# A fused attention, routed-expert and gated-layer kernel: the first keys' queue, four zero matmuls, routing's maxima, one gather's transposes, a split yload and an earlier conversion

## The chip, the core and the metric

The kernel runs on one core of a Trainium2 chip. The metric is device microseconds (us) from the first to the last instruction of one execution with its surroundings; the median of several runs is compared. The core has five engines with their own instruction queues: TensorE (PE, with its weight loads listed apart as PEld), VectorE (DVE), ScalarE (ACT), GpSimd (POOL) and SyncE (SP, which here only asks for DMA transfers). Rows of the profile give times from the start of the span; L12 is line 12 of the kernel before.

## What is computed

Three stages in a row, on 8 batches of 8 heads with 576 tokens and head size 64, so 4608 tokens of 512 features:

```python
a = softmax(phi, axis=2)                      # 8 x 8 x 576 x 32
k_m = einsum('bhsm,bhsd->bhmd', a, k)         # 32 memory rows for each head
v_m = einsum('bhsm,bhsd->bhmd', a, v)
attn = softmax(q @ k_m.T / 8) @ v_m           # x: 4608 x 512

logits = normalised(x) @ normalised(expert_emb).T / tau
e = argmax(logits); gate = softmax(logits)[e]
out = gate * (relu(x @ w1[e]) @ w2[e])        # 8 experts, 512 -> 1024 -> 512

g = out @ w_gate                              # 512 -> 1536
result = (silu(g) * (out @ w_val)) @ w_out    # 1536 -> 512
```

The weights of the last stage arrive as 64-bit floats; all else is 32-bit.

## The kernel before

**Attention (0 to about 240 us).** Batches run staggered, 16 us apart. For one batch: `fetch` (L216) asks SP for phi, k, v and q, four DMAs for each tensor (L223); `weigh` (L245) makes the softmax of phi over the tokens (maxima on VectorE at L251, transposes L257 on TensorE, the subtraction L268, the exponentials on ScalarE at L271); `memory` (L285) multiplies the weights with k and v (L296), then VectorE builds the divisor (L303, L304), a masked copy rm (L306) and the scaled keys km (L313, L314), which TensorE transposes (L320); `queries` (L352) transposes q (L360, L362); `scores` (L370) and `attend` (L405) follow, with the long matmuls at L446 and the copies X<-x at L447. GpSimd's L403 divides the attention weights in one large operation.

**Routing.** For every second batch `route` (L463) takes the maxima of the logits (L479 to L483 on VectorE), makes a one-hot of the expert (L487) and counts tokens of each expert on TensorE (L491 to L493). `table` turns the counts into 37 slots of 128 tokens, each of one expert.

**Main slots (about 240 to 690 us, 12.5 us each).** `moe` (L734): `gather` fetches the 128 rows of a slot (L745), `trx` (L801) transposes them on TensorE (L806) and splits them into a high part xh (ScalarE, L809) and a low part xl (VectorE, L810); `split` (L781) does the same with the expert's weights (w1h L785, w1l L786) where the expert changes; `l1` (L813) multiplies (L820), `trh` (L828) transposes and splits the hidden row (L835 to L839, low part hl), `l2` (L841) multiplies again (L848), `put` (L851) scales and scatters the rows (L854 to L856). A product is made of three matmuls, high by high, high by low and low by high. In the shadow of the slots a converter (L660) turns the 64-bit weights into 32-bit ones, a unit at a time, on VectorE and GpSimd (L666 to L674), and stores them. In slots 17, 19 and 21 `yload` (L1090) prepares 256 rows of the gated layers each: transposes, sums L1104, and then the same split in two parts, L1110 to L1113 for the sources and L1115, L1116 for four sums of them.

**Gated layers (about 690 to 1550 us).** Six blocks of 768 tokens; `fload` (L984) asks for converted weights F, `fsplit` splits them into G0h and G0l (L993, L994), `product` multiplies (L1009), `after` and `both` combine (L1018 to L1055), the sigmoid is at L1046.

**What sets the order.** All instructions are issued in an order written out by hand. In the attention each step is a generator with a due time (`CFG`, one list for each step; `todo` is sorted by it); `moe`'s list says when its first steps come, `warm` is a list of [time, n] for n calls of `busy` (L179), a matmul of zeros into a bank that nobody reads. From slot 1 on, the loop at L906 issues a slot's steps in its own order, with `cv` giving how many conversion units a slot gets. So no planner stands between the code and the queues: an engine does its instructions in the order of the code.

## Time and profile before

| | us |
|---|---|
| median of three timed runs | 1557.24 |
| the three runs | 1557.24, 1552.91, 1561.06 |
| profiled execution, whole | 1552.55 |
| its span, first to last instruction | 1550.8 |
| TensorE busy in it | 1492.7 (96%) |
| mean granted clock of TensorE | 0.976 |

A busy row adds up the durations of an engine's instructions. TensorE's clock is given as granted share: 1.00 is 2.4 GHz, 0.50 is 1.2 GHz. In a timeline row `[1.73 <-DVE km L313]` means that the engine stood idle for 1.73 us before the instruction and that the one named ended last of what it waited for; SPq is SP's queue, in which an issue of a DMA takes the time given. The rows that the prediction uses stand in a section of their own below.

### The profile page before, as it was taken

The page shows a single profiled execution, that of the slowest core. Times are in us where ns is not written, and L with a number is a line of the kernel's source. Part 1 is how long each engine was busy: PE and PEld are TensorE (multiplying, and loading weights), DVE is VectorE, ACT ScalarE, POOL GpSimd, SP SyncE. Part 2 cuts the span into 40 slices and gives each one's busy share as a digit, 9 for nine tenths or more (in the row PEclk, how much of TensorE's full clock was granted, in tenths as well). Part 3 has the DMA queues.
Part 4 walks back from the last instruction along what each step waited for, and adds up shares of the span by engine and source line. Part 5 has one row for each costly group of instructions (what it writes and reads, how often), then busy time and mean ns, then how long its engine had stood idle before and what let it go on. Part 6 is the DMA issues. An engine that isn't in the chain of part 4 may idle for free.

```text
span 1550.8 us, 24891 instructions
## 1 busy us (share of the span) xinstructions
PE 1492.7 (96%) x8362; PEld 1322.8 (85%) x8362; DVE 968.3 (62%) x1632; ACT 706.5 (46%) x1238; POOL 547.4 (35%) x430
## 2 busy tenths in 40 slices
PE   7988789999999999999999999999999999999997
PEld 5777668888877888888988998999899889989996
DVE  5788646856586456635666666566656656765662
ACT  2465653333353242425554554454455444545542
POOL 2345533533332333322243234324332442343233
PEclk8799889999999999999999999999999999999999
DMA  9797535555663364525325323432343244324311
GB/s 311 238 285 174 163 83 188 145 185 169 221 234 118 123 229 148 205 85 197 119 79 179 121 103 93 183 119 89 132 158 111 90 155 142 106 83 168 118 42 54
DMA packets 114527, 230.55 MB, mean 149 GB/s; under 512 B 11021, under 2 KB 62488, under 8 KB 114384
## 3 DMA queue, kind: packets, MB, share of 16 engines
q1 hardware_dynamic: 104368, 200.01, 39.4%
q0 software_dynamic: 10016, 28.81, 5.7%
q8 instruction: 67, 1.10, 0.3%
q14 instruction: 76, 0.62, 0.1%
HBM read 311.67 MB, written 43.21 MB: 229 GB/s over the span
## 4 chain that ended last, share of the span: by engine, by line
PE 66%; DMA 1%; ACT 0%; issue 0%; DVE 0%; another core or an unknown queue 0%; POOL 0%; POOLq 0%; ACTq 0%
PE s L1009 10%; PE k L1009 10%; PE x L1009 10%; PE s L820 5%; PE x L848 5%; PE t L1009 5%; PE k L1201 2%; PE k L1202 2%; PE x L1202 2%; PE k L1200 2%; PE x L1201 2%; PE x L1200 2%; PE s L1201 2%; PE s L1200 2%; PE s L1202 2%; PE t L1100 1%
## 5 line engine op out<-in xcount | busy, mean ns | idle before, releaser
L994 POOL TENSOR_TENSOR G1l<-F,G1h 128x768 fp32r<-128x768 f32 x71 | 140.2, 1975 | 321.6 <-ACT G1h L993 321.5
L1189 POOL TENSOR_TENSOR wo<-wos,wo 128x512 fp32r<-128x512 f32 x72 | 117.4, 1638 | 197.1 <-ACT wo L1188 197.1
L994 DVE TENSOR_TENSOR G0l<-F,G0h 128x1024 fp32r<-128x1024 f32 x72 | 94.2, 1308 | 113.1 <-ACT G0h L993 112.9
L1192 DVE TENSOR_TENSOR uh<-u,uh 128x768 fp32r<-128x768 f32 x72 | 108.0, 1506 | 65.8 <-ACT uh L1191 65.8
L839 DVE TENSOR_TENSOR hl<-t,hh 128x512 fp32r<-128x512 f32 x74 | 47.6, 686 | 118.8 <-ACT hh L838 118.5
L848 PE MATMUL x<-w2h,hh 128*128 128x512 f32 x288 | 117.0, 406 | 0.0
L848 PE MATMUL x<-w2l,hh 128*128 128x512 f32 x288 | 114.2, 396 | 0.0
L848 PE MATMUL x<-w2h,hl 128*128 128x512 f32 x288 | 114.2, 396 | 0.0
L826 ACT ACTIVATE hs<-s 128x512 f32<-128x512 f32 x74 | 40.3, 596 | 145.1 <-PE s L820 138.4
L856 POOL DMA_INDIRECT yd<-y,yi x37 | 40.2, 1088 | 178.7 <-ACT hh L838 128.6
L820 PE MATMUL s<-w1l,xh 128*128 128x512 f32 x296 | 95.1, 403 | 7.7 <-DVEq L783 4.1
L820 PE MATMUL s<-w1h,xh 128*128 128x512 f32 x296 | 97.7, 412 | 2.5 <-ACTq L783 2.5
L820 PE MATMUL s<-w1h,xl 128*128 128x512 f32 x296 | 94.2, 400 | 0.0
L670 POOL TENSOR_TENSOR ca<-ca,cr 128x512 int32<-128x512 int32 x36 | 50.6, 1405 | 116.3 <-DVE cr L669 115.1
L854 ACT ACTIVATE y<-x,tg 128x512 f32<-128x512 f32 x36 | 24.8, 690 | 137.0 <-PE x L848 129.2
L1188 ACT CAST wo<-wos 128x512 fp32r<-128x512 f32 x72 | 45.1, 627 | 67.9 <-PE s L1202 47.8
L993 ACT CAST G0h<-F 128x1024 fp32r<-128x1024 f32 x72 | 75.7, 1052 | 0.7 <-DMA F<-wst 0.5
L820 PEld LDWEIGHTS s<-w1l,xh 128*128 128x128 f32 x296 | 56.7, 193 | 22.7 <-DVEq L783 5.4
L1035 DVE TENSOR_TENSOR u<-u,sg 128x768 f32<-128x768 f32 x72 | 54.4, 755 | 32.9 <-ACT sg L1046 32.9
L1018 ACT COPY s<-s 128x384 f32<-128x384 f32 x72 | 34.6, 481 | 79.8 <-PE s L1009 79.8
L820 PEld LDWEIGHTS s<-w1h,xl 128*128 128x128 f32 x296 | 56.4, 190 | 13.9
L993 ACT CAST G1h<-F 128x768 fp32r<-128x768 f32 x72 | 60.4, 839 | 12.0 <-PE s L1009 12.0
(308 smaller groups left out, 4535.9 us busy)
## 6 DMA issues: line engine op xcount, KB each, us to landing
rw<-in_moe_w_dram SPq DMA_DIRECT2D x296, 512.0 KB
F<-wst SPq DMA_DIRECT2D x71, 896.0 KB
wos<-woc SPq DMA_DIRECT2D x72, 256.0 KB
yt<-yd SPq DMA_DIRECT2D x36, 260.0 KB
xs<-X SPq DMA_DIRECT2D x32, 256.0 KB
cr<-in_moe_w_gate_dram SPq DMA_DIRECT2D x12, 512.0 KB
cr<-in_moe_w_val_dram SPq DMA_DIRECT2D x12, 512.0 KB
wst<-cs SPq DMA_DIRECT2D x12, 512.0 KB
```

What stands on the lines that cost most here:

```text
L670: G.tensor_tensor(out=a, in0=a, in1=lo, op=ALU.add)
L820: PE.matmul(ph[nh], lhsT=l[:, c, :], rhs=r[:, 512 * nh:512 * nh + 512], start=(c == 0 and r is wh and l is xh), stop=(c == KD - 1 and l is ...
L848: PE.matmul(py, lhsT=l[:, c % 4, :], rhs=r, start=(c == 0 and l is hh and r is wh), stop=(c == KF1 - 1 and l is hl))
L993: A.copy(out=h, in_=src)
L994: (G if part and i else V).tensor_tensor(out=l, in0=src, in1=h.bitcast(F32), op=ALU.subtract)
L1009: PE.matmul(pg, lhsT=w[:, k, o], rhs=y[:, RHS[n], k], start=(n in (1, 5, 2) and k == j == 0), stop=(last and k == 1 and j == 2), skip_grou ...
L1035: mul = lambda o, x, y: V.tensor_tensor(out=o, in0=x, in1=y, op=ALU.mult)
L1189: G.tensor_tensor(out=wl, in0=w, in1=wh.bitcast(F32), op=ALU.subtract)
L1192: V.tensor_tensor(out=ul, in0=u, in1=uh.bitcast(F32), op=ALU.subtract)
L1200: PE.matmul(po[t], lhsT=uh[:, cols], rhs=wh, start=(f == 0), stop=False)
L1201: PE.matmul(po[t], lhsT=uh[:, cols], rhs=wl, start=False, stop=False)
L1202: PE.matmul(po[t], lhsT=ul[:, cols], rhs=wh, start=False, stop=(f == NF2 - 1))
```

## The change

Eight edits:

1. The first batch's four k loads are asked for by ScalarE instead of SP; the v loads come next on SP. Other batches are as before.
2. The last entry of `warm` goes from no matmul to four, at −3.86 instead of −20.
3. Two steps of `route` and one of `setup` get later times.
4. Two of `moe`'s first steps go from 104.8 to 108.3: the first slot's `trx`.
5. `cv` gives two units to slots 27 and 30, so that the last of the 37 is done one slot sooner; a second unit of a slot is issued behind the splits.
6. `yload` in slots 17, 19 and 21 is issued in two pieces: the second (L1115 and L1116) behind the next slot's splits.
7. A sigmoid of one column at the end of slot 35.
8. In the first block of the gated layers the split of the next weights is issued ahead of `both(0, 6)`.

```diff
@@ -91,9 +91,9 @@
                             -18.88, -18.88, -15.02],
                  'queries': [-23.63, -23.63, -21.09, -20.21, -19.61],
                  'weigh': [-50.65, -44.65, -42.01, -39.92, -35.01],
-                 'route': [17.41, 23.24, 26.4, 29.17, 30.73, 30.73, 33.02, 34.16, 35.64, 35.64, 35.64, 35.64, 42.66,
+                 'route': [17.41, 23.24, 29.15, 29.17, 31.9, 31.95, 33.02, 34.16, 35.64, 35.64, 35.64, 35.64, 42.66,
                            42.66, 44.07, 44.95, 46.72]},
-        'setup': [-100.87, -100.87, -41.81, -30.12, -26.83],
+        'setup': [-100.87, -50.0, -41.81, -30.12, -26.83],
         'xe': [0, 0, 0, 0, 0, 0, 1, 0, 0, 0],
         'xl': [0, 0, 0, 0, 0, 0, 0, 0, 0, 0],
         'qe': [0, 0, 0, 1, 0],
@@ -102,9 +102,9 @@
         'ee': 1,
         'table': [82.53, 85.4, 88.06, 88.57, 88.57, 92.81, 92.81, 98.9, 98.91],
         'rx': 6,
-        'moe': [89.21, 98.92, 98.93, 100.32, 104.8, 104.8, 116.95, 118.03, 122.94, 123.6, 123.6, 125.1, 125.2,
+        'moe': [89.21, 98.92, 98.93, 100.32, 108.3, 108.31, 116.95, 118.03, 122.94, 123.6, 123.6, 125.1, 125.2,
                 127.15, 127.22, 129.2, 137.62, 137.62, 139.02],
-        'cv': [0, 0] + [1] * 28 + [2] + [1] * 6,
+        'cv': [0, 0] + [1] * 25 + [2] + [1] * 2 + [2] + [1] * 6,
         'tg': 8,
         'ta': 8,
         'cr': 2,
@@ -114,7 +114,7 @@
         'route1': [15.39, 20.26, 21.86, 27.7, 29.44, 29.44, 29.44, 29.44, 32.94, 34.52, 34.52, 34.52, 34.52, 34.52,
                    36.63, 36.63, 44.15],
         'la': 2,
-        'warm': [[-94.73, 10], [-29.6, 0], [-21.65, 0], [-26, 0], [-24, 0], [-20, 0]],
+        'warm': [[-94.73, 10], [-29.6, 0], [-21.65, 0], [-26, 0], [-24, 0], [-3.86, 4]],
         'base': [0.0, 16.0, 32.0, 48.0, 64.0, 79.98, 95.98, 111.98],
         'ke': 0,
         'be': 1}
@@ -213,14 +213,14 @@
         L = {}
         HS = [slice(0, 64), slice(64, 128)]
 
-        def fetch(t, src, b):
+        def fetch(t, src, b, q=SP):
 
 
             for x in range(2):
                 for g in range(2):
                     rows = src[b, 4 * g:4 * g + 4].rearrange("r (p c) d -> p r c d", c=NC)
                     u, c = slice(0, 5 - x) if g == 0 else slice(5 - x, NC), slice(0, 5 - g) if x == 0 else slice(5 - g, NC)
-                    SP.dma_start(out=t[x::2, :, u].rearrange("p r c d -> p r (c d)"), in_=rows[:, :, c].rearrange("p r c d -> p r (c d)"))
+                    q.dma_start(out=t[x::2, :, u].rearrange("p r c d -> p r (c d)"), in_=rows[:, :, c].rearrange("p r c d -> p r (c d)"))
 
         def load_phi(b):
             L["ph", b] = t = ld[b % 3 == 1].tile([P, 4, NC, M], F32, tag=f"ph{b % 3}", name="ph")
@@ -228,7 +228,7 @@
 
         def load_kv(b):
             L["kv", b] = t = ld[b % 2].tile([P, 2, 4, NC, D], F32, tag="kv", name="kv")
-            fetch(t[:, 0], k, b)
+            fetch(t[:, 0], k, b, A if b == 0 else SP)
             fetch(t[:, 1], v, b)
 
         def load_q(b):
@@ -924,7 +924,7 @@
                 fetched[0] += 1
             more(t, 0)
             mid(t, None)
-            conv[1](nu)
+            conv[1](min(nu, 1))
             if more_to_come:
                 trx(t + 1)
                 yield
@@ -934,6 +934,7 @@
                 split1(t + 1)
             more(t, 1)
             exn = expert(t + 2) if t + 2 < NMAIN else None
+            mid(t, 2)
             if exn:
                 load1(t + 2, *exn)
             if t == 0:
@@ -946,6 +947,7 @@
             trh(t)
             split2(t)
             more(t, 4)
+            conv[1](nu - 1)
             if t + 1 < NMAIN:
                 load2(t + 1, *ex)
             ex = exn
@@ -1118,6 +1120,8 @@
     def ahead():
         product(0, 1)
         product(0, 5)
+    sums = []
+
 
     def mid(t, end):
         if 16 <= t < 22 and t % 2 == 0:
@@ -1127,12 +1131,16 @@
                     for sc in scat[TT:]:
                         tc.declare_no_dep(getattr(ld, "ins", ld), getattr(sc, "ins", sc), reason="rows of later tokens")
         if end is None and 16 <= t < 22 and t % 2:
-            for _ in yload(0, (t - 16) // 2, "t"):
-                pass
+            sums.append(yload(0, (t - 16) // 2, "t"))
+            next(sums[0])
+        if end == 2 and sums:
+            next(sums.pop(), None)
         if end == 0 and t in (33, 34):
             fload(0, *((0, 4), (4, 7))[t - 33], pool=spare[0])
-        if end and t == 33:
+        if end == 1 and t == 33:
             fsplit(0, 0)
+        if end == 1 and t == 35:
+            A.activation(out=yp.tile([P, 1], F32, name="tab", bufs=1), in_=half[:, 0:1], func=AF.Sigmoid)
 
     with tc.manual_schedule():
         st_ld, st_wk, st_m, st_c = ExitStack(), ExitStack(), ExitStack(), ExitStack()
@@ -1226,8 +1234,8 @@
                     fsplit(i, 1)
                     after(i, 5)
                     both(i, 2)
+                    fsplit(i + 1, 0)
                     both(i, 6)
-                    fsplit(i + 1, 0)
                     both(i, 3)
                     both(i, 7)
                 elif i == 1:
```

TensorE, at the end of the second batch's memory (L300 closes it, L320 transposes its km, zr is a tile of zeros), the difference:

```order
 L300 MATMUL k<-cs,sm 128x1 x2
 L360 MATMUL t<-cs,q 128x128 x8
+L182 MATMUL x<-zr 128x256 x4
 L320 MATMUL t<-cs,km 128x128 x4
 L362 MATMUL t<-cs,q 64x128 x4
```

The zero matmuls stand between the transposes of the queries and those of km; nothing else moves there.

VectorE, at the first routing (lm and eq are its maxima and their mask, oh the one-hot, rs to km belong to the memory of a later batch), before:

```order
L401 RECIPROCAL smz<-smz 128x36
L479 TENSOR_REDUCE lm<-lg 128x9
L480 TENSOR_TENSOR lg<-lg,lm 128x72
L482 SCALAR_TENSOR_TENSOR eq<-lg,cs 128x72
L483 TENSOR_REDUCE lm<-eq 128x9
L303 TENSOR_SCALAR rs<-k 128x1 x2
L304 RECIPROCAL rs<-rs 128x2
```

and now, further down:

```order
L334 TENSOR_TENSOR vx<-k,rm 128x256 x2
L343 COPY vx<-k 128x8 x2
L479 TENSOR_REDUCE lm<-lg 128x9
L480 TENSOR_TENSOR lg<-lg,lm 128x72
L482 SCALAR_TENSOR_TENSOR eq<-lg,cs 128x72
L483 TENSOR_REDUCE lm<-eq 128x9
L487 TENSOR_TENSOR oh<-lm,cs 128x9x8
```

The four instructions of the maxima went from ahead of the memory's divisor to right ahead of the one-hot.

VectorE in slot 17 (the line of yload's second subtraction is L1116 before and L1118 now, xl and w1l belong to the next slot, hl to this one), before:

```order
L1113 TENSOR_TENSOR yl<-t,yh 128x2x128
L1116 TENSOR_TENSOR yl<-yt,yh 128x8x128
L674 SCALAR_TENSOR_TENSOR ca<-cr,ca 128x512
...
L671 TENSOR_SCALAR cr<-cr 128x512
L810 TENSOR_TENSOR xl<-k,xh 128x512
L779 TENSOR_LOAD new_89
```

and now:

```order
L1115 TENSOR_TENSOR yl<-t,yh 128x2x128
L674 SCALAR_TENSOR_TENSOR ca<-cr,ca 128x512
...
L671 TENSOR_SCALAR cr<-cr 128x512
L810 TENSOR_TENSOR xl<-k,xh 128x512
...
L783 UNCONDITIONAL_BRANCH x2
L1118 TENSOR_TENSOR yl<-yt,yh 128x8x128
L839 TENSOR_TENSOR hl<-t,hh 128x512 x2
```

The large subtraction went from ahead of the conversion unit, xl and the four w1l splits to behind them.

## Rows read from the trace of the kernel before

**Rows 1.** The page: engines' busy time, share of the span, instructions.

```profile
PE 1492.7 (96%) x8362; PEld 1322.8 (85%) x8362; DVE 968.3 (62%) x1632; ACT 706.5 (46%) x1238; POOL 547.4 (35%) x430
```

**Rows 2.** Timeline at the start: start, us, engine, operation, [idle before <-releaser].

```profile
5.07 2.59 SPq L223 DMA_DIRECT2D kv<-in_k_dram  x4
...
7.71 2.59 SPq L223 DMA_DIRECT2D kv<-in_v_dram  x4
...
14.78 0.65 PE L296 MATMUL k<-kv,ph 128*32 128x128 f32 x8 [5.02 <-DMA ph<-in_phi_dram]
```

**Rows 3.** Stretches: us, busy PE PEld DVE ACT POOL, PEclk, DMA share, GB/s.

```profile
6.00:7.00 1.00, 1.00 (x7) 0.87 (x6) 0.65 (x1) 0.00 (x0) 0.00 (x0) 1.00 0.67 110
...
10.00:11.00 1.00, 0.00 (x0) 0.00 (x0) 1.00 (x3) 0.00 (x0) 0.00 (x0) 1.00 1.03 360
```

**Rows 4.** Timeline where the second batch's memory ends.

```profile
40.84 2.13 POOL L403 TENSOR_TENSOR s<-s,smz 128x1152 f32<-128x1152 f32 x1 [8.56 <-DVE rs L303]
...
41.12 1.87 DVE L306 TENSOR_TENSOR rm<-cs,rs 128x12 f32<-128x12 f32 x1
...
43.40 0.91 PE L320 MATMUL t<-cs,km 128*128 128x128 f32 x4 [1.73 <-DVE km L313]
```

**Rows 5.** Stretches: the same 99 matmuls in batches 2 and 3.

```profile
45.45:61.67 16.22, 16.22 (x99) 14.25 (x95) 8.91 (x19) 3.98 (x11) 2.20 (x3) 0.50 0.65 214
...
71.17:80.01 8.84, 8.84 (x99) 7.82 (x95) 8.44 (x19) 3.64 (x10) 1.31 (x1) 1.00 0.96 319
```

**Rows 6.** Timeline: zero matmuls at the start; a later batch's keys.

```profile
1.53 6.01 PE L182 MATMUL x<-zr 128*128 128x256 f32 x20 [1.53 <-POOL zr L176]
...
64.78 1.49 SPq L223 DMA_DIRECT2D kv<-in_k_dram  x2
```

**Rows 7.** Timeline where routing's maxima stand now.

```profile
103.92 2.20 POOL L403 TENSOR_TENSOR s<-s,smz 128x1152 f32<-128x1152 f32 x1 [8.59 <-DVE lm L479]
...
104.17 2.05 DVE L482 SCALAR_TENSOR_TENSOR eq<-lg,cs 128x72 f32<-128x72 f32 x1
...
107.92 0.91 PE L320 MATMUL t<-cs,km 128*128 128x128 f32 x4 [2.40 <-DVE km L313]
...
111.84 0.41 PE L491 MATMUL t<-oh,cs 128*128 128x72 f32 x2 [0.62 <-DVE oh L487]
```

**Rows 8.** Timeline of the first slot's gather and what follows.

```profile
191.63 4.63 DVE L786 TENSOR_TENSOR w1l<-rw,w1h 128x1024 fp32r<-128x1024 f32 x4
...
195.29 1.11 PE L806 MATMUL k<-cs,x 128*128 128x128 f32 x4 [4.72 <-DMA x<-xs,gi]
...
202.45 0.41 PE L491 MATMUL t<-oh,cs 128*128 128x72 f32 x2 [0.84 <-DVE oh L487]
```

**Rows 9.** TensorE's waits, 240 to 690: us in total, times, longest.

```profile
PE s L820 <- DVEq L783: 3.8, 2, 2.0
...
PE s L820 <- DVE w1l L786: 3.6, 1, 3.6
```

**Rows 10.** Timeline of slot 17; stretches behind slot 17's and 21's waits.

```profile
437.15 1.23 DVE L1116 TENSOR_TENSOR yl<-yt,yh 128x1024 fp32r<-128x1024 f32 x1 [0.20 <-ACT yh L1115]
...
446.00:447.00 1.00, 1.00 (x3) 0.79 (x3) 1.00 (x2) 0.00 (x0) 0.85 (x1) 0.50 0.61 241
...
504.00:505.00 1.00, 1.00 (x4) 0.71 (x3) 0.96 (x4) 0.00 (x0) 0.81 (x1) 0.50 0.69 266
```

**Rows 11.** Timeline at the change to the gated layers.

```profile
697.57 0.19 POOL L855 COPY y<-tg 128x8 f32<-128x8 f32 x1 [5.55 <-DMA x<-xs,gi]
...
697.60 1.73 SPq L984 DMA_DIRECT2D F<-wst  x3
...
703.25 1.28 ACT L1046 ACT_TABLE_LOAD   x1
...
704.99 0.85 ACT L1046 ACTIVATE sg<-u 128x768 f32<-128x768 f32 x1 [0.46 <-DVE u L1043]
...
707.34 0.50 PE L1009 MATMUL x<-yh,G1h 128*128 128x384 f32 x1 [1.82 <-DVE u L1041]
```

## The prediction

> **What bounds the kernel now.** I read the page's busy times first: TensorE is busy 96% of the span [rows 1]. So a microsecond is won only where TensorE waits, or where it runs at the lower of its two clock levels (granted 0.50, 1.2 GHz, against 1.00, 2.4 GHz). The views for that are TensorE's waits by stage and the granted clock by stretch. From 240 to 690 the waits view has two rows, 7.4 us in all, and all of it stands in front of the main slots' L820 matmuls for the low halves of the weights [rows 9]; I place them with the timeline in slots 17, 19 and 21. Before 240 the waits are of 0.3 to 5 us, and the change touches four of them: the start [rows 2], the end of the second batch's memory [rows 4], the first routing [rows 7], the first gather [rows 8]. Behind 690 there is one wait of 1.82 us [rows 11]. The clock costs more than the waits: the same 99 matmuls take 16.22 us in batch 2 at 0.50 and 8.84 us in batch 3 at 1.00 [rows 5].
>
> **Part 1, first keys on ScalarE's queue.** SP issues the four k pieces in 2.59 us from 5.07 and the four v pieces behind them, from 7.71 to 10.30; TensorE's first memory matmul comes at 14.78 after 5.02 us of idleness [rows 2]. The row names a phi load as releaser, but the first batch's softmax was done by then, so I read it as the keys and values landing. With k on the other queue v is asked for 2.6 us sooner. That is the upper bound, and the DMA rows cut it: from 10 us on the share is 1.03 at 360 GB/s, so there the bytes set the end, and only the slack ahead counts, 0.33 of a microsecond in 6 to 7 [rows 3] and about 1.5 us in all over 2 to 10. Against it, k now shares the engines with phi, whose maxima VectorE waits for. Bounds 0 and −3, value **−1.5**, nearest to the slack. ScalarE's own queue holds the table load and one small activation behind the four issues; both have over 3 us to spare before its exponentials.
>
> By the Trainium skill ("Trainium Kernel Development and Optimization", Key Constraints) loads from the several queues run on the same 16 DMA engines and interleave, and more queues save only the issue time; by that rule alone the gain is at most SP's issue time, and the saturated row agrees.
>
> **Part 2, four matmuls on zeros.** TensorE ends the second batch's query transposes at 41.67 and starts the transposes of km at 43.40, idle 1.73 us; VectorE's L306 took 1.87 us there while GpSimd's L403 ran [rows 4]. The clock falls 2 us after that gap, at about 45.4, and comes back at 62.5; it is the longest wait of this batch. Four calls are eight records. Twenty records took 6.01 us at the start, the first of them slow [rows 6]: at most 0.30 each and 2.4 us for eight. They wait for nothing, so they fill the gap of 1.73 and put the km transposes off by 0 to 0.7 us; I take 0, since the later ones of those twenty came closer together. If the clock holds, the 99 matmuls take 8.84 instead of 16.22: **−7.4** [rows 5]. Is there cover that would eat this? The next loads of keys wait for batch 2's memory to free a buffer and are issued at 64.78, right behind its last matmul [rows 6], and the DMA had been idle for nine microseconds: they come sooner by the same amount. VectorE has 7.5 us idle in 45 to 62. So the gain carries on into batch 3. For the hold: batch 3 does the same work behind gaps under 0.6 us and stays at 1.00. Against it: in batch 2 mostly transposes and small matmuls surround the filler, where batch 3 has the long attention matmuls. Ends 0 and −7.4.
>
> The Trainium skill ("TensorE: Matmul & The Clock Gate", Part 4: PE-mode transpose) states that transposes don't count as busy for the clock in the way matmuls do. By it the fall could come in spite of the filler, and the sum would lose its largest term (the second case below); no row here separates the two.
>
> **Part 3, routing's maxima later.** VectorE's L482 took 2.05 us because it ran under GpSimd's L403 (103.92 to 106.12); behind it come L303, L304, L306 and km, and TensorE waits 2.40 us, to 107.92 [rows 7]. With L479 to L483 gone from here, L306 comes up under the same L403 and is held itself until 106.12, as in [rows 4]; km is then done about 1.3 us sooner. But the four instructions, about 1.0 us, now stand right ahead of the one-hot L487 for which TensorE already waits 0.62 us until 111.84 [rows 7]: 1.3 of the lead less 1.0 of added work leaves **−0.4**. Ends −1.3 and +0.5.
>
> The Trainium skill ("SBUF — State Buffer", Who interferes with whom) says that a VectorE instruction with two inputs in SBUF contends with a GpSimd one that reads SBUF, and whoever comes first blocks the other for its whole length. Both stretched instructions here fit, and the rule speaks against this part: it only changes which one is held.
>
> **Part 4, the first slot's transposes of x behind 18 attention matmuls.** TensorE waits 4.72 us for the gathered x, to 195.29 [rows 8]. Now it does 18 of the attention matmuls first, and the wait seems gone. But VectorE has no pause from 186.3 to 202.3 (four w1l splits of 4.63 us in all stand in it), and TensorE waits for its one-hot at 202.45 anyhow [rows 8]. So the idle time moves behind the attention matmuls. The clock may then be low there for 3 us longer. Between −1.5 and +2.5, value **+0.5**.
>
> **Part 5, yload in two pieces.** In slots 17, 19 and 21 VectorE's L1116 (1.23 us, and 0.20 idle ahead) stands ahead of the conversion, of xl and of the w1l splits for which TensorE waits [rows 9, 10]. It goes behind the splits, in each of the three slots; ScalarE's cast of 1.06 us likewise. The chain moves up by 1.34 us in each, less than any of the waits (3.57, 2.0, 1.8): 3 × 1.34 = **−4.0**. Behind the waits of slots 17 and 21 the clock is at 0.50 [rows 10], for some 3.4 us each, but not behind slot 19's: about 1.65 us lost for each. With 0.46 left slot 21's fall should go; slot 17 keeps 2.23 us, more than slot 19 had without a fall. One fall gone for sure and half of the other: **−2.4**. What is late next: the moved L1116 now stands ahead of hl (L839), which starts at the same time as before (−1.34 and +1.23), so nothing.
>
> **Parts 6 to 8, at 690.** The conversion ends a slot sooner (the last unit's L674 and store leave 692), Sigmoid's table is loaded in slot 35, and the split of G0 goes ahead of one copy. The F load is issued at 697.60, 0.03 us after GpSimd's L855 at 697.57, which stands behind the landing of the last scatter, not behind the conversion; the table load at 703.25 takes 1.28 us but the sigmoid then waits 0.46 us for u; TensorE waits to 707.34 [rows 11]. u stands on G0h, G0l and F, all unmoved: **0**. The extra conversion units stand in slots 27 and 30, behind the splits, where [rows 9] has no wait (both of its rows end by 502): 0, and some 3 us of VectorE time if that cover were gone. Bounds −3 (F gated by SP) and +1.
>
> **Sum.** −1.5 −7.4 −0.4 +0.5 −4.0 −2.4 = −15.2. The profiled execution took 1552.55 us (span 1550.8): 1552.55 − 15.2 = 1537.3. It is a low one; the median of the three timed runs is 1557.24, and 1557.24 − 15.2 = 1542.0. The mean of all four is 1555.9, which gives 1540.7. I predict **1541**.
>
> **Rivals.** *A: the clock falls in batch 2 all the same*, or at the next gap of the earlier timeline. For it: the surroundings of the filler (part 2). Against: the gap is the only one over 0.6 us there. Sum −15.2 + 7.4 = −7.8: 1548. *B, slower: new falls in batches 3 to 8.* These batches run at 1.00 with gaps of 1 to 2.4 us in them (the 2.40 at 107.92 [rows 7]); when the timeline shifts, such a gap may be followed by the lower clock, and each fall ahead of the small matmuls costs 7.4 us [rows 5]. From −7.8 it decides from the second fall on (−7.8 + 14.8 = +7, 1563); a third gives +14, 1570. Against: part 3 shortens that gap. *C: the loads do not gain and the yload waits are only moved*, the w1l splits being held by the weights' arrival or by ScalarE's w1h casts instead: −7.4 and −2 left, 1546. *D: the F load does come sooner*, being held by the conversion's store through SP: −3 more, 1538.
>
> The Trainium skill (the same clock page, What's actually happening) has the clock judged in windows that run free of the program, so that a gap of one length can be followed by a fall in one execution and not in the next; that is a reason for B and for A, and rows of slots 19 and 21, with waits of 2.0 and 1.8 us and only the shorter followed by a fall, agree.
>
> **How the numbers follow.** Forecast 0.56, D 0.06, C 0.10, A 0.22, B 0.06. Faster or slower by over 0.5% means under 1549.5 or over 1565 (about what a measurement of this kernel can tell from no change). Forecast, D and C are faster: 0.72, and a fifth of A: 0.76. Slower is most of B: 0.05. The rest, 0.19, is the same. The low end is the sum with its best bounds but without D, near −23: 1533. The high end takes A with the start bringing nothing and the gather costing 1.5: 1551.
>
> **What would show it.** In the new trace: the clock at 1.00 from 41 to 60 and the batch-2 stretch of 99 matmuls under 10 us (part 2); the first memory matmul at 12 to 14.8 (part 1); L306 stretched at 104 and km's wait near 1 us (part 3); a TensorE wait of 3 to 5 us in front of L491 near 190 (part 4); L820 waits of about 2.2, 0.7 and 0.5 us (part 5); the wait at the gated layers still 1.8 us (part 6). A batch-2 stretch at 0.50, or a new stretch of 0.50 in batches 3 to 5, would make the prediction wrong.

## The result, and the profile after

| | us |
|---|---|
| before, median of 8 runs | 1560.06 (1552.91 to 1564.98) |
| after, median of 8 runs | 1546.12 (1541.48 to 1547.76) |
| ratio | 0.990, 95% interval 0.9883 to 0.9917 |
| profiled execution after, its span | 1546.46, 1544.7 |
| mean granted clock, profiled executions before and after | 0.976, 0.976 |

The change makes the kernel 1.0% faster: 15.6 us by the ratio (12.9 to 18.3). The forecast was 15.2 us. The two profiled executions are only 6.1 us apart, because the one before was the lucky end of its runs, and their clock is the same on the whole: each has 68.3 us at half clock without the stretch at the very end, so what went in one stage came back in another. A second profile of the kernel before (e10, below) shows how much a stage moves with no edit at all. So a stage is read here from several profiles, and a size in time from the timed runs.

**The start** of the changed kernel, timeline (start, us, engine, line, operation, idle time ahead and what ended it):

```profile
0.75 5.84 ACTq L223 DMA_DIRECT2D kv<-in_k_dram  x4
...
7.13 2.59 SPq L223 DMA_DIRECT2D kv<-in_v_dram  x4
...
7.21 1.98 DVE L251 TENSOR_REDUCE mx<-ph 128x128 f32<-128x512 f32 x2 [6.33 <-DMA ph<-in_phi_dram]
...
14.31 0.66 PE L296 MATMUL k<-kv,ph 128*32 128x128 f32 x8 [2.77 <-DMA ph<-in_phi_dram]
```

The keys are asked for at 0.75, the values at 7.13 instead of 7.71 [rows 2]: not 2.6 us sooner, since SP now waits for one of phi's loads to land before it can issue the next, as its waits of this stretch show (us, times, longest):

```profile
SPq L223 <- DMA ph<-in_phi_dram: 1.8, 1, 1.8
```

In the program's order the loads of both queues take turns on eight completion semaphores (counters by which a load reports that it has landed), and each waits for the one eight places before it; for the first of the values that is one of phi's loads, which had landed before SP came to it in the kernel before. The first maxima over phi (L251) start at 7.21 in the timeline above, against 4.90 in that of before:

```profile
4.90 1.04 DVE L251 TENSOR_REDUCE mx<-ph 128x128 f32<-128x512 f32 x1 [4.02 <-DMA ph<-in_phi_dram]
```

The keys' loads now run beside phi's. The first memory matmul comes at 14.31 instead of 14.78; what ends last in front of it is now the softmax (ScalarE's exponentials end at 14.26), and no longer the values, as the prediction read it for before.

**Batch 2**, timeline of TensorE and the stretch (busy time of PE, PEld, DVE, ACT, POOL, then granted clock, DMA share, GB/s) of the matmuls of [rows 5]:

```profile
40.56 1.89 PE L182 MATMUL x<-zr 128*128 128x256 f32 x8
...
42.45 0.91 PE L320 MATMUL t<-cs,km 128*128 128x128 f32 x4
...
44.51:53.37 8.86, 8.86 (x102) 7.84 (x98) 8.45 (x19) 3.38 (x9) 2.18 (x3) 1.00 1.05 346
```

The eight zero matmuls take 1.89 us, the km transposes follow without the wait of 1.73 [rows 4], and the clock stays at 1.00: 8.86 us where [rows 5] has 16.22.

**The first routing**, timeline of all engines, of TensorE, and a stretch behind it:

```profile
95.69 2.13 POOL L403 TENSOR_TENSOR s<-s,smz 128x1152 f32<-128x1152 f32 x1 [8.59 <-DVE rs L303]
...
96.03 1.81 DVE L306 TENSOR_TENSOR rm<-cs,rs 128x12 f32<-128x12 f32 x1
...
98.25 0.91 PE L320 MATMUL t<-cs,km 128*128 128x128 f32 x4 [0.99 <-DVE km L313]
...
103.24 0.41 PE L491 MATMUL t<-oh,cs 128*128 128x72 f32 x2 [1.69 <-DVE oh L487]
...
105.90:119.40 13.50, 13.50 (x85) 11.89 (x87) 7.73 (x24) 2.77 (x7) 4.12 (x4) 0.50 0.60 159
```

Now L306 is the instruction that is held under L403, 1.81 us; TensorE's wait for km falls from 2.40 [rows 7] to 0.99, and its wait for the one-hot rises from 0.62 to 1.69. Behind that the clock is at 0.50 for the whole stretch 105.9 to 119.4, in which it was at 1.00 before.

**The first gather**, TensorE's timeline and the stretch around it:

```profile
187.34 0.38 PE L656 MATMUL t<-cs,tl 11*128 11x11 f32 x2 [5.02 <-DMA tl<-perm,rwi]
...
201.76 0.68 PE L491 MATMUL t<-oh,cs 128*128 128x72 f32 x2 [3.02 <-DVE oh L487]
...
220.16 0.59 PE L446 MATMUL x<-vh,ah 128*128 128x264 f32 x1 [4.37 <-issue]
...
184.00:230.00 46.00, 32.46 (x139) 28.02 (x140) 19.91 (x45) 23.64 (x55) 17.28 (x17) 0.67 0.31 81
```

The wait of 4.72 in front of L806 [rows 8] is gone. Instead TensorE waits 5.02 for the table's gather (L656), 3.02 for the one-hot (L491) and 4.37 among the last scatters (1.92 there before). The stretch is at a mean clock of 0.67. That this is not the edit's doing is shown by e10 below.

**The main slots**, TensorE's waits from 240 to 690 (us in total, times, longest):

```profile
PE s L820 <- DVEq L783: 3.0, 3, 1.9
...
PE s L820 <- DVE w1l L786: 2.2, 1, 2.2
```

The three waits of [rows 9] shrank, to 2.2, 0.6 and 0.4 us, and a new one of 1.95 us came. It is in front of slot 29's first multiplication, behind two conversion units in a row on VectorE, the second one of slot 27 and that of slot 28; timeline:

```profile
580.06 0.69 DVE L674 SCALAR_TENSOR_TENSOR ca<-cr,ca 128x512 f32<-128x512 int32 x1
...
583.09 1.42 POOL L670 TENSOR_TENSOR ca<-ca,cr 128x512 int32<-128x512 int32 x1 [7.70 <-DVE cr L669]
...
584.54 0.69 DVE L674 SCALAR_TENSOR_TENSOR ca<-cr,ca 128x512 f32<-128x512 int32 x1 [1.19 <-POOL ca L670]
...
587.73 0.68 DVE L810 TENSOR_TENSOR xl<-k,xh 128x512 fp32r<-128x512 f32 x1
...
588.53 0.72 PE L820 MATMUL s<-w1l,xh 128*128 128x512 f32 x2 [1.95 <-DVEq L783]
```

The first unit's second half (L674, 584.54) waits 1.19 us for GpSimd's L670; xl (L810) stands behind both units, and TensorE behind xl.

**The change to the gated layers**, timeline:

```profile
686.28 10.32 SPq L986 DMA_DIRECT2D F<-wst  x3
...
695.20 0.19 POOL L855 COPY y<-tg 128x8 f32<-128x8 f32 x1 [5.49 <-DMA x<-xs,gi]
...
697.90 1.07 ACT L995 CAST G0h<-F 128x1024 fp32r<-128x1024 f32 x1
...
700.73 0.85 ACT L1048 ACTIVATE sg<-u 128x768 f32<-128x768 f32 x1 [1.38 <-DVE u L1045]
...
703.09 0.44 PE L1011 MATMUL x<-yh,G1h 128*128 128x384 f32 x1 [1.31 <-DVE u L1043]
```

The row of the F loads spans three: the first is issued at 686.28, 9 us ahead of GpSimd's L855, where [rows 11] has the two side by side, the other two at 695.8 and 696.2, behind the last scatters as before. The cast of G0h starts at 697.90, 4.3 us sooner than before by the clock on the wall and 2 us sooner in the program's own time. TensorE's wait is 1.31 instead of 1.82, and no fall of the clock follows.

### The profile page after: what moved, and what is told of

It reads as the page before. It is cut to its first block, busy times and chain, and to the rows that moved or that the text cites. A ratio compares the mean times of both kernels' runs of the same rounds, so it can differ in the third digit from the quotient of the medians.

```text
span 1544.7 us, 24908 instructions
## 1 busy us (share of the span) xinstructions
PE 1492.1 (97%) x8370; PEld 1321.6 (86%) x8370; DVE 967.5 (63%) x1632; ACT 706.9 (46%) x1239; POOL 548.9 (36%) x430
## 4 chain that ended last, share of the span: by engine, by line
PE 54%; issue 0%; DVE 0%; POOL 0%; ACT 0%; POOLq 0%
PE s L1011 10%; PE x L1011 10%; PE k L1011 10%; PE t L1011 5%; PE k L1210 2%; PE x L1210 2%; PE k L1209 2%; PE k L1208 2%; PE x L1208 2%; PE x L1209 2%; PE s L1210 2%; PE s L1208 2%; PE s L1209 2%; PE t L1102 1%; POOL out_dram L1214 0%
## 5 line engine op out<-in xcount | busy, mean ns | idle before, releaser
L996 DVE TENSOR_TENSOR G0l<-F,G0h 128x1024 fp32r<-128x1024 f32 x72 | 94.2, 1308 | 108.4 <-ACT G0h L995 108.3
L670 POOL TENSOR_TENSOR ca<-ca,cr 128x512 int32<-128x512 int32 x36 | 50.6, 1405 | 112.2 <-DVE cr L669 111.0
```

What stands on the lines that cost most here:

```text
L670: G.tensor_tensor(out=a, in0=a, in1=lo, op=ALU.add)
L996: (G if part and i else V).tensor_tensor(out=l, in0=src, in1=h.bitcast(F32), op=ALU.subtract)
```

## The experiments

Each kernel was timed beside runs of the kernel before on the same chip; the table gives the ratio with its 95% interval, and in us from before's median in that company (1560.1 for the changed kernel, 1559.4 for e1 to e4, 1561.5 for e5 to e8, 1554.0 for e9 to e12).

| kernel | edits of the change that it has | ratio | us |
|---|---|---|---|
| after | all | 0.9900 (0.9883 to 0.9917) | −15.6 |
| e1 | slots and later, none of the attention | 0.9929 (0.9903 to 0.9955) | −11.1 |
| e2 | zero matmuls alone | 0.9957 (0.9943 to 0.9971) | −6.7 |
| e3 | all but yload | 0.9921 (0.9899 to 0.9942) | −12.3 |
| e4 | all, second unit in slot 23 for 27 | 0.9883 (0.9862 to 0.9904) | −18.2 |
| e5 | e4 without the routing | 0.9898 (0.9881 to 0.9916) | −15.9 |
| e6 | e4 without trx(0) | 0.9887 (0.9870 to 0.9905) | −17.6 |
| e7 | e4 without both | 0.9890 (0.9873 to 0.9907) | −17.2 |
| e8 | e7 without the keys on ScalarE | 0.9882 (0.9858 to 0.9906) | −18.4 |
| e9 | e8 without the zero matmuls | 0.9914 (0.9890 to 0.9938) | −13.4 |
| e10 | the kernel before | 1.0007 (0.9987 to 1.0027) | +1.1 |
| e11 | yload alone | 0.9943 (0.9922 to 0.9965) | −8.9 |
| e12 | e8 with a second group of zero matmuls | 0.9883 (0.9858 to 0.9907) | −18.2 |

**e1, no edit of the attention.**

```diff
-'route': [17.41, 23.24, 29.15, 29.17, 31.9, 31.95, ...], 'setup': [-100.87, -50.0, ...]
+'route': [17.41, 23.24, 26.4, 29.17, 30.73, 30.73, ...], 'setup': [-100.87, -100.87, ...]
-'moe': [..., 108.3, 108.31, ...], 'warm': [..., [-3.86, 4]]
+'moe': [..., 104.8, 104.8, ...], 'warm': [..., [-20, 0]]
-            fetch(t[:, 0], k, b, A if b == 0 else SP)
+            fetch(t[:, 0], k, b)
```

> The changed kernel with its four edits of the attention undone (keys on SP, no zero matmuls in batch 2, routing's maxima and the first slot's transposes where they were); the edits of the main slots and behind stay. Theory of the prediction: the attention's edits are worth 8.8 us (start 1.5, clock 7.4, routing 0.4, gather -0.5), so this kernel keeps 6.4 us of the gain: about 7 us faster than before. Rival, from the trace of the changed kernel: the lead of the attention is lost at the first slot's gather, whose chain over GpSimd and the DMA does not come sooner, and the slots and the change to the gated layers are worth 7.3 - 2.2 + 3.5 = 8.6 us; then this kernel is about 8.6 us or more faster than before, and at 240 us it stands where the kernel before stands.

Measured −11.1 us (−7.0 to −15.1). The prediction's share for these edits, 6.4, is just outside; the rival's 8.6 lies inside. What is left for the four edits of the attention is 15.6 − 11.1 = 4.5 us, against the forecast of 8.8; the two intervals are too wide to tell 4.5 from 8.8. At 230 us (the second slot's transposes) its profile is 0.9 us behind the profile before, so all of its gain comes later.

**e2, the zero matmuls alone.**

```diff
-'warm': [[-94.73, 10], [-29.6, 0], [-21.65, 0], [-26, 0], [-24, 0], [-20, 0]]
+'warm': [[-94.73, 10], [-29.6, 0], [-21.65, 0], [-26, 0], [-24, 0], [-3.86, 4]]
```

> The kernel before with the four zero matmuls of batch 2 alone. Theory of the prediction: the clock stays at its upper level in batch 2 and the gain of 7.4 us is carried to the end: about 7 us faster than before. Rival: TensorE gains 7.4 us at 62 us, but the routing table's scatters, the gather behind them and VectorE's weight splits set the time at 190 to 230 us, so that 0 to 3 us are left at 240 us and at the end. A third: the clock falls later instead, in batch 4 or 5, and takes 4 to 7 us back before 130 us.

```profile
41.27 1.89 PE L182 MATMUL x<-zr 128*128 128x256 f32 x8
...
43.16 0.91 PE L320 MATMUL t<-cs,km 128*128 128x128 f32 x4
...
45.00:60.00 15.00, 14.86 (x183) 12.82 (x183) 13.55 (x30) 9.37 (x21) 4.56 (x5) 1.00 0.94 298
```

TensorE's timeline and the stretch behind: no wait, clock 1.00. Measured −6.7 us (−4.5 to −8.9): the 7.4 of the prediction, and more than the 0 to 3 of the rival.

**e3, yload in one piece again.**

```diff
-            sums.append(yload(0, (t - 16) // 2, "t"))
-            next(sums[0])
+            for _ in yload(0, (t - 16) // 2, "t"):
+                pass
```

> The changed kernel with yload in one piece again in slots 17, 19 and 21. Theory (prediction and trace agree): three waits longer by 1.35 us each and the clock's falls behind one or two of them back: 6 to 7.5 us slower than the changed kernel. Rival: the falls of the clock come and go with the phase and only the waits count: 4 us slower.

```profile
PE s L820 <- DVEq L783: 5.8, 3, 2.0
...
PE s L820 <- DVE w1l L786: 3.6, 1, 3.6
```

TensorE's waits from 240 to 690 of this kernel: the 3.6 of slot 17 is back, and the other row is [rows 9]'s 3.8 and the new 1.95 of slot 29. The clock falls behind slots 17 and 21 as before. In its profile the stretch from slot 17 to slot 23 gains nothing on the profile before, where that of the changed kernel gains 7.3 us (the transposes of slot 17 come at 419.33 before and 422.20 after, those of slot 23 at 508.31 and 503.88). The other profiles agree: with yload in two pieces this stretch takes 81.6 to 81.7 us in eight of them and 83.1 in two (e5, e6), where the clock still falls behind slot 17; in one piece it takes 89.0 in three (before, e3, e10) and 87.4 in e2, whose clock doesn't fall behind slot 21. The timed runs tell e3 from the changed kernel by 3.3 us with intervals that overlap, so they bear out the sign at most; e11 gives the size.

**e4, the second unit in slot 23.**

```diff
-'cv': [0, 0] + [1] * 25 + [2] + [1] * 2 + [2] + [1] * 6
+'cv': [0, 0] + [1] * 21 + [2] + [1] * 6 + [2] + [1] * 6
```

> The changed kernel with the second conversion unit in slot 23, which has no weight split behind it, and not in slot 27. Theory of the prediction: the second unit is hidden in either slot: no difference to the changed kernel. Rival, from the trace of the changed kernel: in slot 27 the two units stand behind four splits of second weights and in front of xl, and TensorE waits 1.95 us there; in slot 23 VectorE has the time, so this kernel is about 2 us faster than the changed one and the wait near 588 us is gone.

```profile
PE s L820 <- DVE w1l L786: 2.1, 1, 2.1
...
PE s L820 <- DVEq L783: 1.0, 2, 0.6
```

TensorE's waits from 240 to 690: the 1.95 is gone, the rest is as in the changed kernel. Between the transposes of slots 29 and 30 this profile moves by 12.51 us and that of the changed kernel by 14.73: 2.2 us for the second unit in slot 27. All three profiles with that unit there (after, e1, e3) take 14.7 us from the one to the other, all eleven others 12.5. The timed difference, 2.6 us by the ratios, fits and doesn't prove it.

**e5 to e8, the other edits of the attention taken back one after another from e4.** e5 takes back the routing (three times of `route`, one of `setup`), e6 the first transposes, e7 both, e8 the keys too, each by the lines of e1's diff.

> The kernel of e4_unit_in_23 with routing's maxima back ahead of the memory's divisor. Theory from the traces: with the maxima ahead of the one-hot TensorE waits 1.7 us there and its clock falls at 104 to 106 for 13.7 us in all three profiles that have the edit and in neither without it, so undoing it gives 1.2 - 1.4 us in waits and about 5 us of clock: 4 to 5 us faster than e4 by 130 us. Theory of the prediction: the edit is worth 0.4 us, so this kernel is 0.4 us slower than e4. Rival: the 5 us are gained by 130 us and lost again at the gather behind the routing table, so nothing is left at 240 us.

> The kernel of e4_unit_in_23 with the first slot's transposes of x back in front of the 18 attention matmuls. Theory of the prediction: the edit costs 0.5 us, since the idle time only moves to the one-hot of the last routing: this kernel is 0 to 1 us faster than e4, with the wait for the gather of 4 to 5 us back and the wait for the one-hot under 1 us. Rival: the edit lengthens the half-clock time behind the gather and this kernel is 2 to 3 us faster. Second rival: the edit is worth the wait that it fills and this kernel is 2 to 4 us slower.

> The kernel of e4_unit_in_23 with both the routing's maxima and the first transposes where they were: the zero matmuls and the keys on ScalarE's queue stay of the attention's edits. Theory from the traces: the lead of 7.4 us of batch 2 is kept to 180 us (as with the zero matmuls alone) and 4 of it to 240 us: 4 to 6 us faster than e4. Theory of the prediction: the two edits cancel, as fast as e4.

> As e7_route_trx_back and the first keys on SP again, so that the zero matmuls are the only edit of the attention. Theory of the prediction: the keys on ScalarE's queue are worth 1.5 us, so this is 1.5 us slower than e7. Theory from the trace of the changed kernel: phi shares the DMA with k, VectorE's first maxima come 2.3 us later (7.21 for 4.90), and 0.9 us are left at the first transposes of km: 0.9 us slower at 28 us, and within the noise at the end.

Measured: −15.9, −17.6, −17.2 and −18.4 against e4's −18.2, with intervals of about 3 us to either side. None of the three edits changes the time by an amount that these runs can tell, and every expectation of 4 us or more fell. e5's profile, a stretch behind the first routing:

```profile
100.00:120.00 20.00, 17.77 (x199) 15.01 (x200) 16.51 (x46) 10.11 (x24) 6.87 (x8) 1.00 0.73 215
```

It has the clock at 1.00, as expected. But e7, with the routing back too, has the fall, timeline and stretch:

```profile
100.28 0.91 PE L320 MATMUL t<-cs,km 128*128 128x128 f32 x4 [2.40 <-DVE km L313]
...
100.00:120.00 20.00, 19.03 (x126) 16.70 (x127) 13.71 (x39) 5.96 (x16) 7.26 (x8) 0.65 0.71 227
```

So the fall at 104 to 106 us isn't the routing edit's alone: it came in the four profiles with the edit and the zero matmuls (after, e3, e4, e6), in one of the five with the zero matmuls and without the edit (e7; not in e2, e5, e8, e12), and e9, with neither, has a fall at 113. Where a profile has none there, as e5's, others come later: e5 has 160 to 174. e6's TensorE at the gather:

```profile
186.49 0.38 PE L656 MATMUL t<-cs,tl 11*128 11x11 f32 x2 [3.73 <-DMA tl<-perm,rwi]
...
190.92 1.12 PE L806 MATMUL k<-cs,x 128*128 128x128 f32 x4 [0.42 <-DMA x<-xs,gi]
...
200.92 0.67 PE L491 MATMUL t<-oh,cs 128*128 128x72 f32 x2 [3.27 <-DVE oh L487]
```

The transposes are in their old place, and yet the wait in front of them is 0.42 us, not 4 to 5: the wait stands at L656 (3.73) and at the one-hot (3.27), as in the changed kernel (5.02 and 3.02). So it isn't the place of L806 that decides where TensorE waits. The 4.6 to 4.7 us in front of L806 came only in the profiles of before and e1, in which TensorE reached L656 as late as 188; in the twelve others that wait is under 0.5 us and the one in front of L491 3.0 to 4.5, whether they have the edit or not.

**e9, e8 without the zero matmuls.**

```diff
-'warm': [..., [-3.86, 4]]
+'warm': [..., [-20, 0]]
```

> The kernel of e8_route_trx_keys_back without the zero matmuls: the kernel before in the whole attention, the later edits with the second conversion unit in slot 23. Theory of the prediction: the zero matmuls are worth 7.4 us also in this company, so this is 7 us slower than e8 (about 0.7% slower than e8, 0.993 of before). Rival: the first gather and the last routing hide part of the lead, as the profiles show at 230 us (1 to 4 us left of 7.5), so this is 2 to 4 us slower than e8. By the sum of the yload waits and clock (7.3) and the change to the gated layers (3.4) it should be 10.7 us faster than before.

```profile
43.02 0.91 PE L320 MATMUL t<-cs,km 128*128 128x128 f32 x4 [1.73 <-DVE km L313]
...
45.00:60.00 15.00, 15.00 (x96) 13.23 (x95) 8.89 (x19) 2.99 (x7) 2.27 (x3) 0.50 0.73 243
```

The wait of 1.73 and the half clock are back. Measured −13.4 (−9.6 to −17.1), 5 us less than e8 and than e12 in the same company (medians 1541.63 and 1536.55); the intervals overlap, so 2 to 4 and 7.4 aren't told apart by this pair. e2 is the better measurement, though with none of the other edits beside it.

**e10, the kernel before once more.** No edit.

> The kernel before once more, for a second profile: the profile shown is of an execution of 1552.55 us, under nearly all of its timed runs (median 1560). Theory: the difference of about 7 us lies in TensorE's clock alone, at other gaps of the attention and the gather, since the mean granted clock of its runs goes from 0.968 to 0.976 with the time; the half-clock stretches of this profile then add up to more than the 68.1 us of the first one, unless the execution is a short one again. Rival: the difference lies in waits of equal clock, for the DMA at the gather.

The stretch 184 to 230 of the first profile of before, and of this one:

```profile
184.00:230.00 46.00, 35.16 (x191) 29.45 (x189) 23.53 (x52) 28.88 (x64) 20.28 (x18) 0.85 0.49 129
```

```profile
184.00:230.00 46.00, 33.90 (x158) 28.54 (x159) 19.79 (x44) 22.96 (x54) 19.39 (x18) 0.74 0.40 112
```

The mean clock there is 0.85 in the first profile and 0.74 in this one (0.67 after, 0.77 in e2, 0.87 in e12). In 130 to 180 it is the other way: this execution gained 6 us there. Its half-clock stretches add up to 75.1 us, against 68.3, as the theory expected, but its span is 1552.0, not a long one, so it doesn't show where a 1560 loses its time; that the clock and the time go together is shown by the runs (from 1550.25 at 0.975 to 1562.43 at 0.967 in this group).

TensorE at the gather, and SP and GpSimd at 697, in this second profile:

```profile
189.09 0.38 PE L656 MATMUL t<-cs,tl 11*128 11x11 f32 x2 [7.01 <-DMA tl<-perm,rwi]
...
193.47 1.12 PE L806 MATMUL k<-cs,x 128*128 128x128 f32 x4 [0.38 <-DMA x<-xs,gi]
...
203.51 0.67 PE L491 MATMUL t<-oh,cs 128*128 128x72 f32 x2 [3.26 <-DVE oh L487]
...
696.67 2.17 SPq L984 DMA_DIRECT2D F<-wst  x3
...
696.74 0.19 POOL L855 COPY y<-tg 128x8 f32<-128x8 f32 x1 [5.77 <-DMA x<-xs,gi]
```

The kernel without any edit has the waits of the changed kernel at the gather, and its first F load is issued ahead of L855. The half-clock stretches move from execution to execution of the same kernel, by 5 us and more in one stretch.

**e11, yload alone.** The kernel before with e3's lines the other way, and the call for the second half behind the splits:

```diff
-            for _ in yload(0, (t - 16) // 2, "t"):
-                pass
+            sums.append(yload(0, (t - 16) // 2, "t"))
+            next(sums[0])
+        if end == 2 and sums:
+            next(sums.pop(), None)
```

> The kernel before with yload in two pieces alone. Theory of the prediction: 4.0 us of waits and 2.4 us of clock, 6.4 us faster than before. By the profiles of the kernels with the edit: 7.3 us between 440 and 510 us against the profile of before, in which two of three waits are followed by a fall of the clock. Rival: where a fall is a matter of the execution, fewer than two come in the median one, and only the waits of 4 us are won.

Measured −8.9 us (−5.4 to −12.1): the prediction's 6.4 and the 7.3 of the profiles lie inside, the bare waits of 4 do not.

**e12, five more zero matmuls in the fifth batch.**

```diff
-'warm': [..., [-3.86, 4]]
+'warm': [..., [-3.86, 4], [44.14, 5]]
```

with a bank of their own for the second group.

> The kernel of e8_route_trx_keys_back with five more zero matmuls in the wait of 2.4 us ahead of the fifth batch's transposes of km (at 98 to 101 us). Theory: the fall of the clock at 104 to 106 us, which came in five of the eight profiles with the first zero matmuls, comes from the 2.4 us of waits there, and does not come any more; it costs 5 us each time, so the median is 1 to 3 us lower than that of e8. Rival: the fall is decided elsewhere, or the first gather hides what is won: as fast as e8.

```profile
97.47 2.43 PE L183 MATMUL x<-zr 128*128 128x256 f32 x10
...
99.89 0.91 PE L321 MATMUL t<-cs,km 128*128 128x128 f32 x4
...
100.00:120.00 20.00, 18.66 (x209) 15.90 (x209) 17.73 (x48) 12.01 (x29) 8.99 (x9) 1.00 0.77 232
```

They fill the wait (no idle time in front of the km transposes at 99.89), the stretch 100 to 120 is at 1.00, and this profile is the shortest of all, a span of 1528.5 us. Its next fall is at 131. But the ratio is e8's, 0.9883 against 0.9882, in another company of runs: a gain over e8 isn't shown.

## Why the prediction was right, and where not

**The sum was right** (15.2 forecast, 15.6 measured, 12.9 to 18.3), and so was the direction. The two largest terms hold alone: the zero matmuls 6.7 (4.5 to 8.9) for 7.4, yload 8.9 (5.4 to 12.1) for 6.4. That the sum came within 0.4 us is in good part luck: by e1 the slots and later gave 11.1 for the forecast 6.4, which leaves 4.5 for the attention's 8.8, and two terms put at 0 were wrong with opposite signs. One sign that the prediction named for being wrong did come: a new stretch at 0.50 in batches 3 to 5 (105.9 to 119.4, behind the fifth batch's km transposes).

**Part 2, right.** The gap is filled, the clock holds in every profile with the zero matmuls (after, e2 to e8, e12) and in none without (before, e1, e9, e10, e11). That is the fall of [rows 5] tied to the gap of [rows 4] by experiment. From the second to the third batch's km transposes it takes 17.3 us in each of the nine profiles with them and 24.5 to 25.4 in the five without: 7.3 to 8.1 us won, forecast 7.4. The rule on transposes of the Trainium skill ("TensorE: Matmul & The Clock Gate", Part 4: PE-mode transpose) would have allowed rival A; it didn't come, with the clock at 1.00 from 45 to 60 in e2.

**That the gain carries on** is shown by the timed runs of e2 alone (6.7 us); in the company of the other edits it isn't told apart from 2 to 4 us (e9). The single profiles tell it badly. The km transposes of batch 3 start at 67.94 before and 59.72 after, but the second slot's at 229.86 and 232.75: read alone, the pair of profiles says that the attention gave back all. More profiles don't settle it: the transposes of slot 17, ahead of the first yload, start at 415.1 to 422.5 in the eight with the first zero matmuls alone and at 417.3 to 422.1 in the five without, with a mean of 419.4 in both. So where the 6.7 us go through the gather isn't shown, and how much of them the whole change keeps stays open. The first profile of before ran the stretch 184 to 230 at 0.85, its second at 0.74. The step that the prediction missed here is that one profile of before isn't its median in such a stretch; it used the profile's low time only for a shift of the whole. Rival B's premise, that batches 3 to 8 ran at 1.00, was misread. Two stretches of before:

```profile
141.00:148.00 7.00, 6.42 (x53) 5.68 (x57) 6.55 (x21) 2.75 (x6) 2.03 (x2) 0.51 0.90 196
171.00:178.00 7.00, 5.75 (x39) 4.78 (x39) 2.34 (x9) 2.66 (x6) 3.48 (x3) 0.55 0.78 211
```

Its mechanism, a new fall in batches 3 to 8, did show in the changed kernel's profile, at 106, and cost some 3 us there (the km transposes of batches 5 and 6 are 9.67 and 5.43 us ahead of before's, and 1.07 of the difference is the longer wait for the one-hot). Whether the routing edit makes it likelier stays open: four of four profiles with it and the zero matmuls, one of five without it.

**Part 1, sign as forecast, size over.** −0.9 us at the first km transposes instead of −1.5, because phi's maxima came 2.3 us later and the softmax now ends last; over all profiles these transposes start at 25.6 to 27.1 with the edit and at 26.1 to 27.8 without, 0.8 sooner in the mean, and the timed runs (e7 and e8) can't see it. The Trainium skill ("Trainium Kernel Development and Optimization", Key Constraints) states that loads of all queues share the same DMA engines; the row of L251 at 7.21 agrees.

**Part 3, right in its steps.** L306 took L482's place under L403 (1.81 us); the first wait lost 1.41, the second gained 1.07: −0.34 for −0.4. Timed, e5 can't see so small a term.

**Part 4, number met, mechanism not shown.** TensorE waits 3.02 us at L491, where 3 to 5 were forecast, but not because of the edit: e6 without the edit waits 3.27 there and the unedited kernel in its second profile 3.26. The wait of 5.02 at L656 was not forecast, and is no mark of the change either: with 7.01 the unedited kernel waits longer. What the three have in common is that TensorE came to the table's gather sooner (at 182.1 to 182.8, in the first profile of before at 188.1). So the term of +0.5 was read from one execution, and no run tells what the edit is worth.

**Part 5, right, a little small.** Waits of 7.4 became 3.2 (2.2, 0.6, 0.4: 4.2 won, forecast 4.0). Both falls of the clock went, where the prediction counted one and a half: 7.3 us in the profile for 6.4. The half had its reason: slot 21's fall went in all ten profiles with the edit, slot 17's in eight.

**Parts 6 to 8, wrong, twice.** The forecast was 0 with bounds −3 and +1. First, slot 27's second unit costs 2.2 us: the step was "behind the splits, where rows 9 has no wait". The absence of a wait showed that one unit fits, not that two do. Two units in a row stall on GpSimd's add (1.19 us), and slot 27 has the four splits of second weights besides. e4 takes the unit elsewhere, and the wait goes. Second, the first F load came 11 us sooner and TensorE's time from 695 to 713 shrank by 3.5 us: 1.5 in three waits and the rest in the clock. For the 200 matmuls from the transposes of the last slot on TensorE takes 41.8 to 41.9 us in all ten profiles with parts 6 to 8, 45.4 to 46.0 in three of the four without, and 44.1 in e2, where the clock doesn't fall there. The step was "the F load stands behind L855, not behind the conversion". Its row at 697.60 came 0.03 us after the start of L855, which by its own 0.19 us ended only behind it; in e10 the load is issued even 0.07 us ahead of that start. What stood in front of it was the branch on SP behind the last store of 692.99: in all four profiles without these edits the load comes 4.6 to 4.7 us behind that store. With the store sooner, the first load went out 9 us ahead of L855. This was rival D. What the sigmoid's table and the order of G0h add to it was not run by itself; with the table loaded sooner the sigmoid waits 1.38 us for u, so u is what it waits for, as forecast.

**The range.** Its low end, 1533, was named as the sum without D near −23. The best bounds of the other terms add up to about −20 (−3 −7.4 −1.3 −1.5 −4.0 and −2.4 to −3.3), so −23 has D in it. The measured time doesn't come near this end.

## What to carry to other kernels

Two rows that start within 0.1 us of each other are no proof that one released the other: check that the first one ended before the second began, or read a second profile, before calling a term zero. A place without a wait has room for what stands there, not for a second one; count the engine's free time in that slot, with the splits that come only in some slots. In a kernel whose clock falls and rises, take two profiles of the kernel before a stage's time is used as a baseline, and try zero matmuls in short gaps ahead of long runs of small matmuls: here four calls kept the clock up in nine profiles of nine, and alone they were worth 6.7 us.

## What the runs showed of the hardware

The half-clock stretches of one and the same kernel move between executions: 184 to 230 us at a mean clock of 0.85 and 0.74 in two profiles of before, and a fall at 109 in one that the other lacks. With equal instructions the timed runs of one group spread over 12 us, and the longest ran at the lowest mean clock (1550.25 at 0.975, 1562.43 at 0.967).

Two VectorE operations on 128x12 and 128x72 elements, L306 and L482, took 1.81 to 2.05 us under GpSimd's L403, and 0.17 and 0.23 us at their shortest elsewhere in before.
